# A fused attention and two-layer kernel: written order on all engines up to slot 20, weight tiles in two overlapped steps, constant products in the start

## The chip, the core and the metric

The kernel runs on one core of one Trainium2 chip. The metric is the device time of one launch in microseconds (us). The engines are TensorE (PE, matrix products; PEld is its loading of stationary operands), VectorE (DVE), ScalarE (ACT), GpSimd (POOL) and SyncE (SP), which here issues all transfers; SPq is SP's queue of transfers. Each engine works through its own list of instructions in order, and semaphores hold an instruction back until its inputs are written and its buffer is free.

## The reference

A linear attention is followed by a normalization and two layers. Token counts: 4 batches of 576 tokens, 8 heads of 64, so 2304 tokens of 512 numbers.

```python
kv  = np.einsum('bhsd,bhse->bhde', k, v)          # 64x64 per head, no softmax
out = np.einsum('bhsd,bhde->bhse', q, kv)
rms = np.sqrt(np.mean(out * out, axis=-1, keepdims=True) + 1e-06)
x   = (out / rms * g_norm)                        # to (2304, 512)

h = x @ w_in                                      # layer 1: 512 -> 2048
g = h * np.tanh(softplus(h))                      # mish
x = g @ w_out                                     # 2048 -> 512

h = x @ w_in2                                     # layer 2, same shapes
g = np.maximum(h, 0) + alpha * np.minimum(h, 0)   # a slope per hidden unit
return g @ w_out2
```

The weights of both layers come as 64-bit floats, everything else as 32-bit floats.

## The kernel before

**Blocks and slots.** The 2304 tokens are cut into blocks of 512, 256, 512, 512 and 512 (block 0 to block 4). Layer 1 takes the blocks in this order, layer 2 in the order 0, 2, 3, 4, 1. For each block the 2048 hidden units are done in 16 chunks of 128 (index j), so there are 2 x 5 x 16 = 160 steps, called slots: slots 0 to 15 are block 0 of layer 1, slots 16 to 31 block 1, and so on. In slot s, `slot` issues the first product of chunk s (`mm1`, 12 matmuls into the tile `h`), the activation of chunk s-1 (`mish` on ACT, or `prelu` on DVE in layer 2) and the second product of chunk s-4 (`mm2`, 12 matmuls added into the `acc` tiles; LAG = 4).

**Three matmuls for one.** Each product operand is split in a high part and a low rest. `three` (L121) multiplies high by high (L122), high by low (L123) and low by high (L124). So each operand is made in two operations: a copy to the high type on ACT (`xh` L306, `w` L381, `gh` L115) and a subtraction on DVE (`xl` L311, `w` L385, `gl` L118). In before the split of g (`g_split`) is issued directly behind the activation.

**Weight tiles.** A tile of 64-bit weights is loaded as pairs of 32-bit words into a staging buffer `ws` (`load_w`, L325 for `w_out`, L328 and L330 for `w_in`; three buffers). It is turned into a 32-bit tile `wf` by a scaling on ACT (`w_scale`, L336) and three operations on DVE, each reading the result of the one before (`w_bits`: L342, L343, L346); the text calls these three a bit build. Then come the high copy on ACT (`w_high`, L381) and the low subtraction on DVE (`w_low`, L385). `prep_w` issues the four steps of one tile. In slots 4 to 15 each slot prepares a tile of `w_in` (called w with its j) and one of `w_out` (u with its j), in the group `last`, at the end of the slot. The tiles c0 to c3 are the `w_in` tiles for j = 0 to 3, laid out as `w1first`.

**Attention.** The 512 columns of x are four pairs of heads. For block i and pair p: load of q (L175) and, for a new batch, of k and v (L153); `kv_pe` makes kv (L191), `kv_ev` copies its two 64x64 corners to SBUF (L199 on ACT, L200 on DVE); `t_pe` transposes q (L209, L211), `t_ev` copies it (L218, ACT); `o_pe` multiplies (L226). Block 0 then goes through a square (L240), a product with constants that gives the mean over each head (L244), a root on ACT (L249, L252) and three DVE operations. For blocks 1 to 4 the means of all four pairs are gathered, `rsqrt_ev` finds the reciprocal root by a bit trick and three Newton steps on DVE (twelve operations, L276 to L285, the last writes `yr`), and four broadcast products (`b_pe`, L290) and scalings (`b_ev`, L296) give x. The table `WHEN` puts these steps of block i+1 as `hook`s into half-slots of block i; the loads go to `pre`, two slots ahead of the transpose but not before slot 4.

**What sets the order.** Everything before slot 4 is under a manual schedule of all engines: the loads in the order of the string `FIRST` (p is k, v and q of a pair; c, w, u are weight tiles), then the steps of the string `START`, one letter for a step (k for kv, t for transpose, o for the output product, A, D, H, L for the four weight steps, P for `mm1`, x and y for the two halves of x, g for `mish`) and its indices. From slot 4 on only PE's order is the written one; on the other engines a scheduler with a model of times chooses, and it may place a later slot's instructions among those of the start.

## Time and profile before

| | us |
|---|---|
| median of 3 runs (912.61 to 913.68) | 912.66 |
| the profiled execution | 913.11 |
| its span, first to last instruction | 911.30 |
| PE busy in the span (95%) | 865.6 |
| DVE busy (48%) | 440.3 |
| ACT busy (31%) | 281.8 |
| POOL busy | 1.4 |
| read from and written to HBM | 52.44 and 9.44 MB |

The profile is of one execution. Its times count from the first instruction; the span leaves out 1.8 us that lie around it. Busy is the time in which an engine executes an instruction; waits are not in it. The profile page cuts the span into 40 slices of 22.8 us and gives the busy share of each in tenths: PE begins with 6, 4, 7, 8, 9, 7, 7 and stands at 9 from then on, so the time in which PE isn't busy lies in the first seven slices, some 160 us. The views by stretch, by wait and by instruction below go there.

### The profile page before, as it was taken

Reading aid. Unit: us, or ns where it says so; the run is one execution under the profiler, and the core shown is the slowest. Engines: PE = TensorE matmul, PEld = TensorE weight load, DVE = VectorE, ACT = ScalarE, POOL = GpSimd, SP = SyncE. Lnnn points to the kernel's source line nnn. Section 1 sums busy time; section 2 is a strip of 40 time slices with the busy share of each in tenths; the row PEclk is TensorE's granted clock in tenths of the full one; section 3 lists DMA queues with packets and bytes.
Section 4 is the critical chain, followed back from the end, with each engine's and each line's share of the span. In section 5 each row is a group of like instructions: output and inputs, shape, how many; then the busy total and the mean of one; then the engine's idle time right before and its main releaser. Section 6 shows DMA issues by size and latency. Waiting matters only on the chain.

```text
span 911.3 us, 10793 instructions
## 1 busy us (share of the span) xinstructions
PE 865.6 (95%) x4368; PEld 709.8 (78%) x4368; DVE 440.3 (48%) x760; ACT 281.8 (31%) x513; POOL 1.4 (0%) x11
## 2 busy tenths in 40 slices
PE   6478977999999999999999999999999999999998
PEld 3356766898887887788888888888888888888897
DVE  4277787125114413351677789544344433444444
ACT  2364654333322334232555344111112111111111
POOL 0000000000000000000000000000000000000000
PEclk9789998999999999999999999999999999999999
DMA  9604852340310003000454144011002000100010
GB/s 244 198 1 133 250 175 67 76 123 1 91 46 12 1 17 122 1 0 24 161 164 142 65 165 159 1 36 58 1 1 81 0 1 1 59 1 0 1 47 24
DMA packets 50753, 62.57 MB, mean 69 GB/s; under 512 B 19728, under 2 KB 41232, under 8 KB 50704
## 3 DMA queue, kind: packets, MB, share of 16 engines
q1 hardware_dynamic: 50704, 61.89, 22.5%
q8 instruction: 34, 0.56, 0.3%
q14 instruction: 15, 0.12, 0.0%
HBM read 52.44 MB, written 9.44 MB: 68 GB/s over the span
## 4 chain that ended last, share of the span: by engine, by line
PE 86%; DMA 6%; DVE 4%; SPq 2%; ACT 1%; issue 1%; DVEq 0%; ACTq 0%
PE acc L122 14%; PE h L122 14%; PE h L124 14%; PE acc L123 14%; PE h L123 14%; PE acc L124 14%; DMA ws<-in_moe_w_in_dram 2%; DMA ws<-in_moe_w_out_dram 2%; SPq L175 2%; PE ops L226 1%; PE kvps L191 1%; DMA v<-in_v_dram 1%; DMA q<-in_q_dram 1%; DVE wf L346 1%; DVE wf L343 1%
## 5 line engine op out<-in xcount | busy, mean ns | idle before, releaser
L118 DVE TENSOR_TENSOR gl<-n,gh 128x512 fp32r<-128x512 f32 (+1 forms) x160 | 102.0, 637 | 347.2 <-ACT gh L115 346.8
L115 ACT CAST gh<-n 128x512 fp32r<-128x512 f32 (+1 forms) x160 | 92.3, 577 | 384.8 <-PE acc L123 243.3
L122 PE MATMUL h<-xh,w 128*128 128x512 f32 (+1 forms) x480 | 180.9, 377 | 2.6 <-ACT w L381 2.6
L124 PE MATMUL h<-xh,w 128*128 128x512 f32 (+1 forms) x480 | 178.6, 372 | 0.6 <-DVE w L385 0.4
L123 PE MATMUL h<-xl,w 128*128 128x512 f32 (+1 forms) x480 | 178.2, 371 | 0.0
L122 PE MATMUL acc<-gh,w 128*128 128x512 f32 (+1 forms) x320 | 120.9, 378 | 0.4 <-ACT w L381 0.4
L124 PE MATMUL acc<-gh,w 128*128 128x512 f32 (+1 forms) x320 | 118.2, 369 | 0.0
L123 PE MATMUL acc<-gl,w 128*128 128x512 f32 (+1 forms) x320 | 118.1, 369 | 0.0
L122 PE MATMUL acc<-w,gh 128*128 128x512 f32 x288 | 112.2, 390 | 0.0
L123 PE MATMUL acc<-w,gh 128*128 128x512 f32 x288 | 112.2, 390 | 0.0
L124 PE MATMUL acc<-w,gl 128*128 128x512 f32 x288 | 112.0, 389 | 0.0
L122 PEld LDWEIGHTS h<-xh,w 128*128 128x128 f32 x480 | 91.4, 190 | 21.6 <-issue 3.4
L124 PEld LDWEIGHTS h<-xh,w 128*128 128x128 f32 x480 | 91.5, 191 | 17.5 <-DVE w L385 2.2
L123 PEld LDWEIGHTS h<-xl,w 128*128 128x128 f32 x480 | 91.6, 191 | 15.9 <-issue 0.5
L122 PEld LDWEIGHTS acc<-gh,w 128*128 128x128 f32 x320 | 60.6, 189 | 11.0 <-ACT w L381 0.7
L124 PEld LDWEIGHTS acc<-gh,w 128*128 128x128 f32 x320 | 60.5, 189 | 10.7 <-DVE w L385 0.4
L123 PEld LDWEIGHTS acc<-gl,w 128*128 128x128 f32 x320 | 60.6, 189 | 10.2 <-issue 0.5
L336 ACT ACTIVATE ws<-ws 128x512 f32<-128x512 f32 x64 | 43.3, 681 | 68.6 <-DMA ws<-in_moe_w_out_dram 37.2
L122 PE MATMUL h<-xh,w1first 128*128 128x512 f32 (+1 forms) x160 | 62.8, 392 | 1.3 <-ACT xh L306 1.3
L124 PEld LDWEIGHTS acc<-w,gl 128*128 128x128 f32 x288 | 54.1, 188 | 11.3
L122 PEld LDWEIGHTS acc<-w,gh 128*128 128x128 f32 x288 | 54.2, 188 | 10.9
L123 PE MATMUL h<-xl,w1first 128*128 128x512 f32 (+1 forms) x160 | 60.6, 379 | 2.2 <-DVE xl L311 2.2
(80 smaller groups left out, 845.8 us busy)
## 6 DMA issues: line engine op xcount, KB each, us to landing
ws<-in_moe_w_in_dram SPq DMA_DIRECT2D x32, 512.0 KB, 4.5
ws<-in_moe_w_out_dram SPq DMA_DIRECT2D x32, 512.0 KB, 3.5
k<-in_k_dram SPq DMA_DIRECT2D x16, 288.0 KB, 4.1
v<-in_v_dram SPq DMA_DIRECT2D x16, 288.0 KB, 4.3
out_dram<-osb SPq DMA_DIRECT2D x18, 256.0 KB, 2.4
x2d<-xs SPq DMA_DIRECT2D x8, 512.0 KB, 2.7
xs<-x2d SPq DMA_DIRECT2D x8, 512.0 KB, 4.2
q<-in_q_dram SPq DMA_DIRECT2D x16, 128.0 KB, 3.5
```

Of the source, the lines that this page charges most:

```text
L115: nc.scalar.copy(out=hi, in_=src)
L118: lo_eng.tensor_tensor(out=lo, in0=src, in1=f32(hi), op=ALU.subtract)
L122: nc.tensor.matmul(ps, lh, rh, start=start, stop=False)
L123: nc.tensor.matmul(ps, lh, rl, start=False, stop=False)
L124: nc.tensor.matmul(ps, ll, rh, start=False, stop=stop)
L175: nc.sync.dma_start(out=t[p0 : p0 + n, h, :, :], in_=q[b, 2 * p + h, s : s + C * n, :].rearrange("(p c) d -> p c d", c=C),)
L191: nc.tensor.matmul(ps[hs, hs], kt[:, h, j, :], vt[:, h, j, :], start=(j == 0), stop=(j == KVJ - 1))
L226: nc.tensor.matmul(cols(ps), kv_of(b, p), cols(qT), start=True, stop=True)
L336: nc.scalar.mul(high, high, 2.0**-112)
L343: nc.vector.scalar_tensor_tensor(out=si, in0=high, scalar=-0x80000000, in1=si, op0=ALU.bitwise_and, op1=ALU.bitwise_or)
L346: nc.vector.scalar_tensor_tensor(out=si, in0=high, scalar=3, in1=si, op0=ALU.logical_shift_left, op1=ALU.bitwise_or)
```

## The change

1. A constant `MANUAL` = 20: slots 4 to 19 are now issued inside the manual schedule of all engines; from slot 20 on, as before, only PE's order is written.
2. `prep_w` is cut in two: `w_begin` does scaling and bits of a tile and then ends the tile begun before it (`w_end`: high and low). In slots 4 to 15 the `w_in` tile is begun in a new group `mid` (after the activation, before `mm2`), the `w_out` tile in `last`; so the high and low of one tile stand behind the bits of the next.
3. `g_split` of a chunk is no longer issued behind its activation but one slot later, after `mm2`. `split` is gone (its two lines stand in `g_split`).
4. `START` and `FIRST` are written anew. In `START` PE steps and evacuations now have letters of their own (K and k, T and t, O, M, G), and W with a number issues so many matmuls of a constant 128x128 tile with itself (14 in all: W9, W2, W2 and one more); nothing reads their result. In `FIRST` pair 1 comes before tile c1 as before but pair 2 behind it; the load of `gcol` moves behind pair 1.
5. `kv_ev` copies both corners on DVE for block 0 and both on ACT for the others (before: one on each).
6. The loads of q, k and v of pairs 1 to 3 of a block are issued in the slot after the half-slot in which the previous pair's kv step stands, no longer two slots ahead of the transpose.

```diff
-FIRST = "p0 c0 p1 p2 c1 p3 c2 c3 w4 u0 w5 u1".split()
+MANUAL = 20
+FIRST = "p0 c0 p1 c1 p2 p3 c2 c3 w4 u0 w5 u1".split()
 START = """
-k0 t0 Ac0 o0 Dc0 s0 m0 Hc0 k1 l0 Lc0 n0 t1 f0 o1 k2 s1 x0 m1 Ac1 y0 l1 Dc1 P00 P01 P02 P03 n1 Hc1
...
+W9 K0 k0 W1 T0 t0 W2 Ac0 O0 Dc0 s0 W2 K1 M0 k1 Hc0 Lc0 T1 l0 t1 n0 O1 f0 K2 s1 x0 M1 k2 Ac1 y0 T2 l1
...
     def kv_ev(b, p):
         ps = at.pop(("kv", b, p))
-        nc.scalar.copy(out=kv_of(b, p)[:D, :D], in_=ps[:D, :D])
-        nc.vector.tensor_copy(out=kv_of(b, p)[D:, D:], in_=ps[D:, D:P])
+        for hs in (slice(0, D), slice(D, P)):
+            if b == 0:
+                nc.vector.tensor_copy(out=kv_of(b, p)[hs, hs], in_=ps[hs, hs])
+            else:
+                nc.scalar.copy(out=kv_of(b, p)[hs, hs], in_=ps[hs, hs])
...
+    begun = []
+    def w_end():
+        while begun:
+            w = begun.pop()
+            w_high(*w)
+            w_low(*w)
+    def w_begin(*w):
+        w_scale(*w)
+        w_bits(*w)
+        w_end()
+        begun.append(w)
...
-        g_split(kk, g)
+        gs[kk] = g
...
-            add(pre, max(h // 2 - 2, EARLY), load_q, i, p)
+            before = max((h - step + dk) // 2 + 1 if p else h // 2 - 2, EARLY)
+            add(pre, before, load_q, i, p)
...
-            add(last, j - 2, prep_w, 0, 1, j)
+            add(mid, j - 2, w_begin, 0, 1, j)
...
-            add(last, j + 2, prep_w, 0, 2, j)
+            add(last, j + 2, w_begin, 0, 2, j)
+            add(mid, j + 3, w_end)
...
             prelu(s - 1)
+        run(mid, s)
         run(fin, s)
         if s - LAG >= 0:
             mm2(s - LAG)
+        if s - 2 < K:
+            g_split(s - 2)
         run(hook, 2 * s + 1)
...
+    def warm(n):
+        ps = bank("acc3", "warm")
+        for _ in range(n):
+            nc.tensor.matmul(ps[:, :P], ones_bd, ones_bd, start=True, stop=True)
...
+        begun.append((0, 2, 1))
+        for s in range(EARLY, MANUAL):
+            slot(s)
     with tc.manual_schedule(engines={mybir.EngineType.PE}):
-        for s in range(EARLY, K + LAG):
+        for s in range(MANUAL, K + LAG):
             slot(s)
```

Three places show how instructions move. The first is ACT in the start, around the copy of the third transposed q (L218 before, L216 now), between the root of pair 1 and the high half of that pair's or the next pair's x. Before:

```order
L252 ACTIVATE u<-q 128x512
L381 CAST w1first<-wf 128x4x128
L336 ACTIVATE ws<-ws 128x512 x2
L218 COPY q<-tps 128x512
L336 ACTIVATE ws<-ws 128x512
L199 COPY kv_102<-kvps 64x64
L336 ACTIVATE ws<-ws 128x512
L306 CAST xh_346<-q 128x512
```

Now:

```order
L247 ACTIVATE q<-mps,epsb 128x512
L250 ACTIVATE u<-q 128x512
L216 COPY q<-tps 128x512
L238 ACTIVATE q<-ops 128x512
L379 CAST w1first<-wf 128x4x128
L304 CAST xh_349<-q 128x512
L334 ACTIVATE ws<-ws 128x512
```

Before, two scalings of staged weights stand ahead of the copy; now the copy stands right behind the root, and the scaling of the next tile comes after the high half of x.

The second place is SP, the transfers from slot 4 on: `w_out` and `w_in` tiles, and q (four pieces), k and v of block 1's pairs. Before:

```order
L325 DMA ws<-in_moe_w_out_dram 128x1024 x2
L328 DMA ws<-in_moe_w_in_dram 128x4x256
L175 DMA q<-in_q_dram 32x2x64 x2
L175 DMA q<-in_q_dram 96x2x64 x2
L153 DMA k<-in_k_dram 96x2x384
L153 DMA v<-in_v_dram 96x2x384
L328 DMA ws<-in_moe_w_in_dram 128x4x256
L325 DMA ws<-in_moe_w_out_dram 128x1024
```

Now:

```order
L323 DMA ws<-in_moe_w_out_dram 128x1024 x2
L326 DMA ws<-in_moe_w_in_dram 128x4x256 x2
L170 DMA q<-in_q_dram 32x2x64 x2
L170 DMA q<-in_q_dram 96x2x64 x2
L148 DMA k<-in_k_dram 96x2x384
L148 DMA v<-in_v_dram 96x2x384
L323 DMA ws<-in_moe_w_out_dram 128x1024
L326 DMA ws<-in_moe_w_in_dram 128x4x256
```

Before, a q stands between the first and the second `w_in` tile of this stretch (j = 6 and 7), and it was pair 2's, as the q of pairs 0 and 1 had been issued ahead of these rows; now both `w_in` tiles go first, and the q behind them is pair 1's.

The third place is DVE in block 0's last slots, around the reciprocal root of block 1 (L276 to L285 before, L274 to L283 now). Before:

```order
L276 TENSOR_SCALAR qT<-msps 128x256
L118 TENSOR_TENSOR gl<-n,gh 128x512
L342 TENSOR_SCALAR wf<-ws 128x512
L277 TENSOR_SCALAR qT<-qT 128x256
L385 TENSOR_TENSOR w_1063<-wf,w_1063 128x512
L343 SCALAR_TENSOR_TENSOR wf<-ws,wf 128x512
L281 TENSOR_TENSOR qT<-qT 128x256
L342 TENSOR_SCALAR wf<-ws 128x512
L346 SCALAR_TENSOR_TENSOR wf<-ws,wf 128x512
L282 SCALAR_TENSOR_TENSOR qT<-qT 128x256
```

Now:

```order
L447 TENSOR_TENSOR gl<-n,gh 128x512
L274 TENSOR_SCALAR qT<-msps 128x256
L275 TENSOR_SCALAR qT<-qT 128x256
L279 TENSOR_TENSOR qT<-qT 128x256
L280 SCALAR_TENSOR_TENSOR qT<-qT 128x256
L281 SCALAR_TENSOR_TENSOR qT<-qT 128x256
...
L283 SCALAR_TENSOR_TENSOR yr<-yr,neglo,qT 128x256
L340 TENSOR_SCALAR wf<-ws 128x512
L341 SCALAR_TENSOR_TENSOR wf<-ws,wf 128x512
L344 SCALAR_TENSOR_TENSOR wf<-ws,wf 128x512
L383 TENSOR_TENSOR w_1020<-wf,w_1020 128x512
```

Before, the steps of the root alternate with bit builds and low halves of weights; now its twelve steps stand in a row, and the three steps of a bit build too.

## Rows read from the trace of the kernel before

**Rows 1.** Windows: busy us (and instructions) per engine, granted clock, DMA share.

```profile
core 0: us, PE busy (x) PEld busy (x) DVE busy (x) ACT busy (x) POOL busy (x), PEclk, DMA share, GB/s
0.00:31.47 31.47, 21.91 (x140) 13.63 (x140) 14.74 (x51) 9.37 (x17) 1.43 (x11) 1.00 0.92 243
31.47:42.85 11.38, 0.00 (x1) 0.00 (x0) 0.00 (x0) 1.77 (x3) 0.00 (x0) 0.70 0.70 212
42.85:65.95 23.10, 18.50 (x84) 12.41 (x85) 15.15 (x25) 14.99 (x26) 0.00 (x0) 0.78 0.00 1
65.95:161.91 95.96, 81.41 (x449) 62.79 (x447) 74.69 (x144) 50.04 (x96) 0.00 (x0) 0.93 0.51 151
161.91:911.30 749.39, 743.78 (x3700) 620.93 (x3696) 335.75 (x542) 205.67 (x372) 0.00 (x0) 1.00 0.16 51
```

**Rows 2.** Waits of PE, whole span: total us, times, longest us.

```profile
PE kvps L191 <- ACT q L218: 11.4, 1, 11.4
PE bps L290 <- DVE yr L285: 11.1, 2, 9.2
PE kvps L191 <- DMA v<-in_v_dram: 5.2, 1, 5.2
```

**Rows 3.** Timeline, ACT around 41 us: start, length, instruction, [idle before it].

```profile
40.37 0.65 ACT L336 ACTIVATE ws<-ws 128x512 f32<-128x512 f32 x1 [12.21 <-DMA ws<-in_moe_w_out_dram]
...
42.23 0.57 ACT L218 COPY q<-tps 128x512 f32<-128x512 f32 x1
```

**Rows 4.** Chain that ended last, first 200 us: start, length, step.

```profile
12.59 8.19 DMA v<-in_v_dram
```

**Rows 5.** Waits of SP's queue, 0 to 160 us: total, times, longest.

```profile
SPq L175 <- PE tps L211: 48.3, 3, 31.7
```

**Rows 6.** Timeline of SP after that wait.

```profile
69.56 2.51 SPq L175 DMA_DIRECT2D q<-in_q_dram  x4
...
77.86 0.39 SPq L328 DMA_DIRECT2D ws<-in_moe_w_in_dram  x1
```

**Rows 7.** Timeline of PE, first matmul of slot 16.

```profile
161.91 0.39 PE L122 MATMUL h<-xh,w1first 128*128 128x256 f32 x1
```

**Rows 8.** Timeline of DVE, one bit build and the next one's start.

```profile
59.39 0.42 DVE L342 TENSOR_SCALAR wf<-ws 128x512 int32<-128x512 int32 x1
59.84 0.69 DVE L343 SCALAR_TENSOR_TENSOR wf<-ws,wf 128x512 int32<-128x512 int32 x1
60.57 0.69 DVE L346 SCALAR_TENSOR_TENSOR wf<-ws,wf 128x512 int32<-128x512 int32 x1
61.18 0.42 DVE L342 TENSOR_SCALAR wf<-ws 128x512 int32<-128x512 int32 x1
```

**Rows 9.** Timeline of PE, two products that give the means of a pair.

```profile
12.87 2.07 PE L244 MATMUL mps<-q,ones_bd 128*128 128x512 f32 x2 [0.69 <-ACT q L240]
...
48.61 1.13 PE L244 MATMUL mps<-q,ones_bd 128*128 128x512 f32 x2 [1.18 <-ACT q L240]
```

**Rows 10.** Timeline of PE after the wait for the root (`yr`).

```profile
142.09 0.63 PE L122 MATMUL h<-xh,w 128*128 128x512 f32 x1
142.52 0.63 PE L123 MATMUL h<-xl,w 128*128 128x512 f32 x1
...
145.64 0.40 PE L122 MATMUL h<-xh,w 128*128 128x512 f32 x1
145.88 0.39 PE L123 MATMUL h<-xl,w 128*128 128x512 f32 x1
```

**Rows 11.** Groups of DVE, 65.95 to 161.91: count | busy us, mean ns | idle before.

```profile
L281 DVE TENSOR_TENSOR qT<-qT 128x256 f32<-128x256 f32 x3 | 1.3, 418 | 0.0
...
L276 DVE TENSOR_SCALAR qT<-msps 128x256 f32<-128x256 f32 x1 | 0.4, 423 | 0.0
```

**Rows 12.** Transfers issued at 94.7 and at 106.8: count, size, us to landing.

```profile
ws<-in_moe_w_in_dram SPq DMA_DIRECT2D x1, 512.0 KB, 4.3
...
ws<-in_moe_w_in_dram SPq DMA_DIRECT2D x1, 512.0 KB, 5.5
```

More of the change, by code (lines that the diff above doesn't have):

```diff
@@ L111, in attn_moe_moe2 @@
     f32 = lambda t: t.bitcast(F32)
-    def split(hi_eng, lo_eng, hi, lo, src):
-        if hi_eng is nc.scalar:
-            nc.scalar.copy(out=hi, in_=src)
-        else:
-            hi_eng.tensor_copy(out=hi, in_=src)
-        lo_eng.tensor_tensor(out=lo, in0=src, in1=f32(hi), op=ALU.subtract)
     def three(ps, lhs, rhs, start, stop):
@@ L385, in w_low, with prep_w @@
         nc.vector.tensor_tensor(out=l, in0=s, in1=f32(h), op=ALU.subtract)
-    def prep_w(L, which, j):
-        for f in (w_scale, w_bits, w_high, w_low):
-            f(L, which, j)
-    hps, gt, acc = {}, {}, {}
+    begun = []
[9 more added lines that the diff above has]
+        begun.append(w)
+    def prep_w(*w):
+        w_begin(*w)
+        w_end()
+    hps, gs, gt, acc = {}, {}, {}, {}
     def at_slot(kk):
@@ L427, in m_tile, with g_split @@
         return mp.tile([P, T], dt, tag=nm, name=nm, bufs=bufs)
-    def g_split(kk, g):
+    def g_split(kk):
         T = at_slot(kk)[3]
+        g = gs.pop(kk)
         gh, gl = m_tile("gh", T, F32R), m_tile("gl", T, F32R)
-        split(nc.scalar, nc.vector, gh, gl, g)
+        nc.scalar.copy(out=gh, in_=g)
+        nc.vector.tensor_tensor(out=gl, in0=g, in1=f32(gh), op=ALU.subtract)
         gt[kk] = gh, gl
@@ L479, in load_x2 @@
         x2s[i, p], x2s[i, p + 1] = xs[:, :T], xs[:, T:]
-    pre, hook, fin, last = ({} for _ in range(4))
+    pre, hook, mid, fin, last = ({} for _ in range(5))
     def add(d, s, f, *a):
@@ L500, in attn_moe_moe2 @@
             if i in new_kv:
-                add(pre, max(h // 2 - 2, EARLY), load_kv, new_kv[i], p)
+                add(pre, before, load_kv, new_kv[i], p)
                 add(hook, h + dk, kv_pe, new_kv[i], p)
@@ L544, in slot @@
             mm2(s - LAG)
+        if s - 2 < K:
+            g_split(s - 2)
         run(hook, 2 * s + 1)
         run(last, s)
+    def warm(n):
+        ps = bank("acc3", "warm")
+        for _ in range(n):
+            nc.tensor.matmul(ps[:, :P], ones_bd, ones_bd, start=True, stop=True)
     code = {"c": 0, "w": 1, "u": 2}
     first = {
-        "k": lambda p: (kv_pe(0, p, "acc0"), kv_ev(0, p)),
-        "t": lambda p: (t_pe(0, p, "acc0"), t_ev(0, p)),
-        "o": lambda p: o_pe(0, p, f"acc{1 + p % 2}"),
+        "W": warm,
+        "K": lambda p: kv_pe(0, p, "acc0"),
+        "k": lambda p: kv_ev(0, p),
+        "T": lambda p: t_pe(0, p, "acc0"),
+        "t": lambda p: t_ev(0, p),
+        "O": lambda p: o_pe(0, p, f"acc{1 + p % 2}"),
         "s": s_ev,
-        "m": m_pe,
+        "M": m_pe,
         "l": m_ev,
@@ L566, in attn_moe_moe2 @@
         "g": mish,
+        "G": g_split,
     }
@@ L575, in attn_moe_moe2 @@
                 load_w(0, code[n[0]], int(n[1:]), True)
-            if n == FIRST[0]:
+            if n == "p1":
                 for h in range(2):
@@ L602, in attn_moe_moe2 @@
             if n[0] in "ADHL":
-                first[n[0]](0, code[n[1]], int(n[2:]))
+                w = (0, code[n[1]], int(n[2:]))
+                first[n[0]](*w)
             else:
                 first[n[0]](*(int(c) for c in n[1:]))
+        begun.append((0, 2, 1))
+        for s in range(EARLY, MANUAL):
+            slot(s)
     with tc.manual_schedule(engines={mybir.EngineType.PE}):
-        for s in range(EARLY, K + LAG):
+        for s in range(MANUAL, K + LAG):
             slot(s)
```

8 lines of the change are left out of this document (4 added, 4 removed).

## The prediction

> **What bounds the kernel now.** I began with the windows [rows 1]. From 161.91 us on TensorE (PE) is busy for 743.78 of 749.39 us: that stretch is matmul work and no order of other engines shortens it. The 161.91 us before it hold 121.8 us of PE work, and that is all a start-up change can reach. The waits of PE [rows 2] name three large items: one wait of 11.4 us for an ACT copy, one of 9.2 us (of 11.1) for the block-1 reciprocal root `yr`, 5.2 us for the first loads.
>
> The timeline around the first [rows 3] shows its real cause: PE waits for ACT's copy of the third transposed q, and that copy stands on ACT behind a weight scaling (L336) that waited 12.21 us for a `w_out` transfer. That tile belongs to a later slot; the order lists show that the scheduler set it into the hand-written start. Meanwhile the last q/k/v of block 0 were long there: the v of pair 3 was issued at 12.59 and landed 8.19 us later, at 20.8 [rows 4].
>
> The SP queue shows a third delay [rows 5]: a q load waited 31.7 us for a PE transpose, and the weight tile for j=7 was issued only at 77.86, behind it [rows 6]. So slots 4 to 15 began with weight tiles late, and VectorE (DVE), which needs about as long per slot as PE, ran 74.69 of 95.96 us there [rows 1].
>
> **The change, part by part.** Marks are slot 4's first matmul (65.95, the edge of a window in rows 1) and slot 16's, 161.91 [rows 7].
>
> *Start, up to slot 4.* With ACT in written order no scaling of a later slot stands ahead of a copy, so the 11.38 us stretch with an idle PE goes. What is late next? Data first: pair 3 is complete at about 21. Then DVE: from about 19 us its list, in written order, holds for pairs 1 to 3 and the tiles c1 to c3: three bit builds, three lows, three normalizations, three x lows and two kv copies. By the distances of the starts in [rows 8] a build is 0.45+0.73+0.61 = 1.79. What else has 512 columns I price by these steps: a low (of a weight, of x or of g) 0.61 to 0.7, a normalization, three dependent operations, 3 x 0.73 = 2.2, a pair of kv copies one short step, 0.5. The sum is 5.4+2.0+6.6+2.0+1.0 = 17 us, to 36 or 37. The low half of x3 is the last of it and releases the last twelve first-layer matmuls, 12 x 0.24 = 2.9 us [rows 10]: slot 4 starts at about 41 instead of 65.95, **25 us less**. Bounds: 26 (no wait left in that list) and 20 (PE's in-order chain of kv, transpose, o and mean products at the lower clock for all four pairs).
>
> *Warm-up products.* 14 products of 128x128 on PE. Before, none exists; by the mean product of 512 columns, 2.07 us at 12.87 and 1.13 at 48.61 [rows 9], a quarter of that is 0.5 or 0.28 us. Nine of them, 2.5 to 4.5 us, stand where PE waits 5.2 us for the first v [rows 2]; they may overrun that by some 0.5 us, on a path that then waits for transfers, so nothing. Five more stand in waits like the 0.69 us at 12.87. What they may give: the two mean products tell that PE ran its first 30 us at the lower of its two levels (1.2 GHz), though the profile writes a granted 1.00 there [rows 1]. At the higher one each pair's PE steps take about half. It is a gain only where PE, not DVE, is last, which after the step above it mostly isn't: 0, bounds -3 and +1, already in the ends of the first term.
>
> *kv copies.* Block 0's go to DVE, the others' to ACT: eight small copies less on DVE (at most a short step each, 3.6 us), beside other work: 0.
>
> *Load order (q and k/v of block 1).* In the written order q of pair 1 stands behind the j=7 tile, q of pair 2 behind j=9, and q of pair 2 finds the buffer that pair 0's transpose frees in slot 4, so the 31.7 us wait goes. But in the built program each `w_in` tile waits for the build of the `w_in` tile before it (the buffer freed first is handed out first), so SP holds the q of pair 2 until tile 8 is built, in the middle of slot 6, and its transpose comes right after the matmuls of slot 7. I walk it below.
>
> *Slots 4 to 15.* Before they take 95.96 us: 14.55 idle, some 14 matmuls at the lower level (0.43 instead of 0.24, 2.7 us in all [rows 10]), 78.6 us of work. After, DVE from its first build of slot 4's tile has 24 tiles (w4 to w15, u0 to u11) of 1.79+0.6 = 57.4 us, twelve `gl` of 0.61 (7.3), the block-1 root with twelve operations (the kinds from L276 to L285, 1.3 busy for each of three of them, 0.4 for a small one [rows 11]; 5.1 in all, 5.6 with gaps) and block 1's four x (3.5): 74 us, from 37 to 111. PE from 41 to 120. Both are nearly full, so each wait of one for the other is lost. Walking the two lists by these pitches: (a) `gh` waits for the second product of its slot, since its buffer is read there, then come `gl`, build u, low w, low u, build w: 5.4 us, within a slot of 5.45 to 6.9; (b) a `w_in` tile lands 4.3 us after its issue [rows 12], then scaling (0.65 [rows 3]) and two bit steps (1.2): 6.2 us from build to build, within a slot while attention steps lengthen it (slots 4 to 9), 0.7 us over it in slots 10 to 13, which the waits of (d) and (e) cover; (c) q of pair 2 issues at about 64, lands at 69, PE is ready at 65.3: 3.7 idle and 1.8 at the lower level after it; (d) in slot 10 the root stands in a row on DVE, between `gl` and the build of u8, so low w12 comes at 105 where PE wants it at 100: 4.5, and 1.5 at the lower level; (e) block 1's four broadcast products and slot 15's weights wait 3 us behind DVE. With 0.5 of small waits that is 78.6+15 = 93.6, less about 2 since the last x tiles overlap slot 15: 91.5, **4.5 us less**. Bounds: 78.6 (PE never waits, -17) and 104 ((b) paces every slot at 8 us, +8).
>
> A rule weighed against this: of the two long bit operations the one whose result the next operation reads takes 0.73 us, the one with another tile's work behind it 0.61 [rows 8]; the written order gives up that mixing, 0.12 us per tile, 3 us over 24 tiles. The Trainium skill (VectorE: DVE Perf Modes, "The DRAIN you can't avoid") says that a semaphore between chained operations costs nothing extra, as the pipeline drains anyway. The rows speak against that by 0.12 us; by the page the DVE sum would be 71 instead of 74.
>
> *From slot 16 on.* The order on PE is the same, and DVE (336 us busy of 749) has room: 0. Bounds: -3.6 (the 1.9 us of the second root's wait and the low level after it gone) and +3 (another such wait, since the split of g now stands after the second product).
>
> Sum: -25 - 4.5 + 0 = -29.5. The profiled execution took 913.11 us (span 911.30), 0.45 above the median of the runs: 913.1 - 29.5 = 883.6, or **883** on the median's footing.
>
> **Rivals.**
> 1. *The two queues mesh.* Items (c) to (e) vanish in the slack: slot 16 at 120, saving 25 + 17 = 42, 871. For: the sums of PE and DVE (79 and 74) allow it. Against: one root on DVE already cost 9.2 us before.
> 2. *The weight path paces slots 4 to 15.* One buffer for all `w_in` tiles, the transfer shared with q and k/v (5.5 instead of 4.3 in one case [rows 12]), scaling behind `gh` on ACT: 8 us per slot, 41 + 104 = 145, saving 17: 896.
> 3. *Slower: TensorE stays at the lower level through slots 4 to 15.* Before, the waits of 11.4 and 9.2 us were each followed by work at the lower level [rows 1, 10]. If every slot has such a wait, the 78.6 us of work take 157: slot 16 at 41 + 157 + 14 = 212, and 50 us are lost: 963. It decides from 30 us of work run at half rate, between four and five of the twelve slots. Against: after such a wait about seven matmuls ran slow, 1.4 us in all. The Trainium skill (TensorE: Matmul & The Clock Gate, "HAM oscillation") describes such a kernel, which falls back at every tile's load wait; the trace shows the fall after single waits, none of a repeated kind.
> 4. *The change doesn't do what it says:* the scheduler puts tiles of slots from 20 on ahead of the written ones, as it did with L336. The order lists of the built program show none; then 900 at best. Too small to count apart from 2.
>
> **Chances and range.** Forecast 0.70 (873 to 892), rival 1 0.13, rival 2 (with 4) 0.13, rival 3 0.04. To hold 8 in 10 the range reaches to the points of both neighbours, 870 to 897, and leaves out their far halves and rival 3, 0.17 in all. Faster 0.95, within 0.2% (1.8 us, about what a measurement here can tell) 0.01, slower 0.04.
>
> **What would show it.** ACT: the copy of the third q right after its transpose, before 30 us. PE: slot 4's first matmul near 41, slot 16's near 132. SP: no wait over 10 us before slot 8, but the q of pair 2 issued after tile 9, and a PE wait at its transpose. DVE: the root's operations in a row, and PE waiting in slot 12. Granted clock: a dip after each of these two waits. Wrong if PE is idle for over 5 us between 6 and 40 other than for transfers, if slot 4 starts after 46, or if new waits stand after slot 16.

## The result, and the profile after

| | before | after |
|---|---|---|
| median of the runs | 912.63 us | 887.15 us |
| lowest and highest | 912.54 to 913.68 | 885.32 to 889.0 |
| the profiled execution, its span | 913.11, 911.30 | 887.53, 885.7 |

The ratio is 0.9718, with a 95% interval of 0.9697 to 0.974: the change saves 25.5 us. The forecast was 883, with a range of 870 to 897. The span lost 25.6 us, and the windows tell where. They answer to [rows 1], now cut at PE's first transpose, at slot 4's first matmul and at slot 16's. The columns are the same: busy us and instructions of PE, PEld, DVE, ACT and POOL, the granted clock, the DMA share and GB/s.

```profile
0.00:12.97 12.97, 5.02 (x44) 4.63 (x45) 4.83 (x36) 1.28 (x1) 1.43 (x11) 0.93 0.89 234
12.97:45.04 32.07, 29.41 (x209) 19.92 (x209) 24.13 (x42) 20.78 (x35) 0.00 (x0) 0.92 0.76 216
45.04:137.86 92.82, 82.38 (x450) 63.85 (x449) 73.45 (x131) 49.92 (x100) 0.00 (x0) 0.94 0.51 149
137.86:885.70 747.84, 742.27 (x3700) 619.36 (x3696) 340.72 (x546) 210.97 (x386) 0.00 (x0) 1.00 0.17 52
```

Up to slot 4 the time fell from 65.95 to 45.04 (20.9 us), slots 4 to 15 from 95.96 to 92.82 (3.1 us), everything from slot 16 on from 749.39 to 747.84 (1.55 us). The prediction had 25, 4.5 and 0.

The 11.4 us wait of [rows 2] for ACT's copy of the third q is gone. That copy stands right behind the root, with no idle time ahead of it (timeline of ACT, answering to [rows 3]):

```profile
26.11 0.63 ACT L250 ACTIVATE u<-q 128x512 f32<-128x512 f32 x1
26.64 0.57 ACT L216 COPY q<-tps 128x512 f32<-128x512 f32 x1
```

What PE waits for now, over the whole span (total us, times, longest us; answers to [rows 2]):

```profile
PE tps L207 <- issue: 6.3, 1, 6.3
PE tps L209 <- DMA q<-in_q_dram: 3.1, 1, 3.1
PE h L117 <- ACT w L379: 2.1, 1, 2.1
...
PE bps L288 <- DVE qT L294: 1.9, 1, 1.9
PE bps L288 <- DVE yr L283: 1.9, 1, 1.9
PE warm L572 <- DVE ones_bd L615: 1.4, 1, 1.4
PE acc L117 <- ACT n L453: 1.4, 1, 1.4
PE h L119 <- DVE w L383: 1.2, 1, 1.2
```

All but the first are short. But for the wait for the second root (`yr`, block 2's, behind slot 16) and the one at the constant products, those shown lie in slots 4 to 15; the rows left out are two of 1.0 us and smaller ones. The first is new and the longest, and its row names no engine that it waits for, only "issue". It stands in PE's timeline at 12.97, ahead of the very first transpose:

```profile
5.32 0.92 PE L186 MATMUL kvps<-v,k 96*64 96x64 f32 x24 [0.21 <-DMA v<-in_v_dram]
6.17 0.49 PE L572 MATMUL warm<-ones_bd 128*128 128x128 f32 x2
12.97 1.97 PE L207 MATMUL tps<-ident,q 128*64 128x128 f32 x16 [6.32 <-issue]
```

DVE's timeline at the same time gives the reason:

```profile
5.29 0.15 DVE L629 TENSOR_TENSOR neglo<-neglo,ident 128x1 f32<-128x1 f32 x1
12.31 0.15 DVE L630 TENSOR_SCALAR gneg<-gcol 128x1 f32<-128x1 f32 x1 [6.88 <-DMA gcol<-in_g_norm_dram]
12.42 0.46 DVE L196 COPY kv<-kvps 64x64 f32<-64x64 f32 x2
```

The product kv was done at 6.2. Its two copies to SBUF are now both on DVE, and they stand there behind `gneg`, a constant made from `gcol`. Point 4 of the change moved the two tiny `gcol` transfers behind pair 1's loads; they were issued at 5.2 and landed at 12.3, in the queue of the large ones. The transpose uses the bank that kv occupies until the copies are done, so DVE, ACT and PE all stood still for 6 us. PE paid for it twice: the kv product ahead of the wait took 0.92 us, the higher of TensorE's two levels, and the transposes behind it 1.97, the lower one (1.09 in the next pair).

### The profile page after: what moved, and what is told of

Same layout as the page of the kernel before. It is cut to its first block, busy times and chain, and to the rows that moved or that the text cites. A ratio compares the mean times of both kernels' runs of the same rounds, so it can differ in the third digit from the quotient of the medians.

```text
span 885.7 us, 10841 instructions
## 1 busy us (share of the span) xinstructions
PE 859.1 (97%) x4396; PEld 707.8 (80%) x4396; DVE 443.1 (50%) x752; ACT 283.0 (32%) x521; POOL 1.4 (0%) x11
## 4 chain that ended last, share of the span: by engine, by line
PE 92%; DVE 3%; ACT 2%; DMA 2%; issue 1%; SPq 0%; DVEq 0%
PE acc L117 15%; PE acc L118 14%; PE acc L119 14%; PE h L117 14%; PE h L119 14%; PE h L118 14%; PE ops L224 2%; PE kvps L186 2%; DMA ws<-in_moe_w_in_dram 1%; PE tps L209 1%; DVE wf L341 1%; DVE wf L344 1%; PE mps L242 0%; DMA v<-in_v_dram 0%; PE bps L288 0%
## 5 line engine op out<-in xcount | busy, mean ns | idle before, releaser
L117 PEld LDWEIGHTS acc<-gh,w 128*128 128x128 f32 x320 | 60.9, 190 | 12.3 <-ACT n L453 1.8
L119 PEld LDWEIGHTS acc<-gh,w 128*128 128x128 f32 x320 | 60.8, 190 | 10.9 <-DVE w L383 0.4
L118 PEld LDWEIGHTS acc<-gl,w 128*128 128x128 f32 x320 | 61.0, 191 | 10.3 <-issue 0.5
L117 PEld LDWEIGHTS acc<-w,gh 128*128 128x128 f32 x288 | 54.1, 188 | 10.7
L118 PEld LDWEIGHTS acc<-w,gh 128*128 128x128 f32 x288 | 54.1, 188 | 10.7
L117 PE MATMUL h<-xh,w1first 128*128 128x512 f32 (+1 forms) x160 | 59.9, 375 | 0.0
```

Source lines behind the costliest of these rows:

```text
L117: nc.tensor.matmul(ps, lh, rh, start=start, stop=False)
L118: nc.tensor.matmul(ps, lh, rl, start=False, stop=False)
L119: nc.tensor.matmul(ps, ll, rh, start=False, stop=stop)
```

## The experiments

All are edits of the kernel after, and each was timed against the kernel before. The "stretch" is the time from slot 4's to slot 16's first matmul in the profiled execution. "PE idle" is the stretch less PE's busy time in it, that is, what PE waited. "Slow" counts the matmuls of 512 columns in the stretch that took over 0.55 us, where the others took some 0.4. The two columns tell a wait that an edit removed from a lower clock that an execution happened to miss.

| run | edit, in words | median us | ratio, 95% interval | slot 4 | stretch | PE idle | slow |
|---|---|---|---|---|---|---|---|
| after | | 887.15 | 0.9718, 0.9697 to 0.974 | 45.04 | 92.82 | 10.4 | 21 |
| e1_gcol_early | `gcol` loaded behind pair 0 | 882.71 | 0.9661, 0.9641 to 0.9681 | 37.65 | 94.42 | 10.3 | 28 |
| e2_manual_to_4 | written order up to slot 4 only | 900.72 | 0.9867, 0.9844 to 0.9891 | 55.46 | 94.60 | 14.6 | 10 |
| e3_no_warm | no constant products | 889.07 | 0.9735, 0.9715 to 0.9754 | 44.52 | 93.73 | 9.9 | 27 |
| e4_one_step | weight tiles in one step | 905.08 | 0.9908, 0.9891 to 0.9926 | 44.02 | 109.95 | 24.0 | 28 |
| e5_gcol_no_warm | e1 without constant products | 883.31 | 0.9684, 0.9668 to 0.9699 | 40.70 | 92.38 | 10.9 | 15 |
| e6_gcol_q_early | e1, q of pair 2 earlier | 880.4 | 0.9653, 0.9634 to 0.9671 | 38.31 | 92.19 | 10.7 | 15 |
| e7_gcol_root_split | e1, root in three parts | 882.57 | 0.9672, 0.9658 to 0.9685 | 37.65 | 93.39 | 11.8 | 12 |
| e8_all_three | e6, e7 and earlier broadcasts | 883.01 | 0.9675, 0.9656 to 0.9694 | 37.98 | 94.48 | 11.2 | 21 |
| e9_two_more_stages | e1, two staging buffers for w_in | 876.25 | 0.9585, 0.9563 to 0.9607 | 37.68 | 87.57 | 7.9 | 8 |
| e10_two_bit_steps | e1, a bit operation left out | 873.22 | 0.9559, 0.9537 to 0.9582 | 38.08 | 85.69 | 5.0 | 14 |
| e11_stages_and_three | e8 and e9 | 876.25 | 0.959, 0.9568 to 0.9611 | 37.55 | 87.75 | 7.5 | 12 |
| e12_waits_one_by_one | e9, three local edits | 874.43 | 0.9579, 0.9564 to 0.9594 | 37.95 | 85.64 | 7.4 | 0 |

### The load that moved with the rest: e1

```diff
-            if n == "p1":
+            if n == "p0":
                 for h in range(2):
                     nc.sync.dma_start(out=gcol[...], in_=g_norm...)
```

> The kernel after, with one edit: the two small gcol transfers stand behind pair 0's loads again (as before the change), not behind pair 1's. Theory A: in the kernel after, DVE's list is held at gneg until gcol lands (12.31 us), the first kv copies stand behind it, and PE has 6.3 us without work; with gcol early gneg comes at 6 to 7 us, everything up to slot 4 moves by 5 to 6 us (slot 4's first matmul at 39 to 40 instead of 45.0), and the time is 881 to 882.5. Theory B: transfers or DVE's sum of work bound the start anyway; slot 4 moves by under 2 us and the time stays at 885 to 888.

Measured: 882.71 us, and slot 4's first matmul at 37.65, 7.4 us earlier. DVE's rows at the place of the 6.88 us wait:

```profile
6.26 0.15 DVE L630 TENSOR_SCALAR gneg<-gcol 128x1 f32<-128x1 f32 x1 [0.81 <-DMA gcol<-in_g_norm_dram]
6.60 0.46 DVE L196 COPY kv<-kvps 64x64 f32<-64x64 f32 x2 [0.18 <-PE kvps L186]
```

Theory A holds for the start, which gained more than its 5 to 6 us. Of the 7.4 us, 4.3 reach the profiled time (883.27 against 887.53): slots 4 to 15 took 1.6 us more and the rest 1.6 us more. Neither is a wait that the edit made: PE waits as long in the stretch as in after (10.3 against 10.4) and has 28 slow matmuls against 21; for the rest see the last section.

### What the written order of the later slots gave the start: e2

```diff
-MANUAL = 20
+MANUAL = 4
```

> The kernel after with MANUAL = 4: START, FIRST, the two-step preparation and the later split of g stay, only the written order of ACT, DVE and SP from slot 4 on is undone. In its order list five scalings of later weight tiles stand again among ACT's steps of the start; DVE's list of the start is unchanged. Theory A: the 11.4 us wait of before was such a misplaced scaling, so one or more waits of ACT of 5 to 15 us come back, PE waits for an ACT copy, slot 4 starts at 55 to 66, the time is 897 to 908. Theory B: the new START list is what gained, and the written order of the later slots little; slot 4 at 45 to 48, the time 886 to 890.

Measured: 900.72 us, slot 4 at 55.46. ACT's timeline has the old picture again, now a pair later: one scaling stands ahead of the fourth copy.

```profile
30.30 0.69 ACT L247 ACTIVATE q<-mps,epsb 128x512 f32<-128x512 f32 x1
38.25 0.66 ACT L334 ACTIVATE ws<-ws 128x512 f32<-128x512 f32 x1 [7.27 <-DMA ws<-in_moe_w_out_dram]
38.81 0.61 ACT L250 ACTIVATE u<-q 128x512 f32<-128x512 f32 x1
39.33 0.57 ACT L216 COPY q<-tps 128x512 f32<-128x512 f32 x1
```

PE's product with that copy waited 6.9 us. DVE's written start is the same as in after, so theory A holds for the 10.4 us by which slot 4 is later: they are this wait and 4.5 us more of PE busy time up to slot 4, at a granted clock of 0.78 from 13 us on where after has 0.92, less 0.9 us by which the wait for `gneg` is shorter. In the stretch the wait for the block-1 root is there again with 10.3 us, and PE waits 14.6 us in all against 10.4; that the stretch is only 1.8 us longer is in part due to fewer slow matmuls (10 against 21). So more than half of what the written order of slots 4 to 19 brings lies in the start, by keeping later work out of it. The other half of the start's 20.9 us comes from the rest of the change: with `MANUAL` = 4 slot 4 is still 10.5 us earlier than in before. Which of its parts gave that (the new `START`, the load order, the copies of kv on one engine) no run separates.

### The constant products: e3 and e5

```diff
-W9 K0 k0 W1 T0 t0 W2 Ac0 O0 Dc0 s0 W2 K1 M0 k1 ...
+K0 k0 T0 t0 Ac0 O0 Dc0 s0 K1 M0 k1 ...
```

> The kernel after without its 14 constant products. Theory A (the prediction's): they are worth nothing, since DVE's list paces the start; slot 4 at 44.5 to 46, the time 886.5 to 888.5. Theory B: PE's chain of transposes and products paces the start (from 13 to 31 us PE has gaps of 1 us only), and without the constant products it runs at the lower level up to about 29 us, as before; each of four pairs takes 2 to 3 us longer, slot 4 at 51 to 55, the time 893 to 897.

Measured: 889.07 us, slot 4 at 44.52 (45.04 with them): theory A for the start. The time lies 0.6 us above its range, with 27 slow matmuls in the stretch against 21, and 1.6 us more from slot 16 on, of which the last section tells. But the reason is not the one given there. In both kernels PE is at the lower level after the wait of some 6 us for `gneg` (the first transposes take 1.97 us in both), so that wait undoes what the products ahead of it had given. e5 takes the wait away.

> gcol early (as in e1_gcol_early) and without the 14 constant products. Theory A: the constant products were worth nothing in the kernel after because the 6 us wait for gneg gave the time back anyway; with that cover gone PE runs the pairs at the lower level (kv step 1.55 instead of 0.92, transposes 1.97 instead of 1.09, o 2.05 instead of 1.10, means 2.07 instead of 1.13), 3.4 us per pair for two or three pairs, until it has worked long enough: slot 4 at 42 to 47 instead of 37.65, the time 887 to 892. Theory B: DVE's list paces the start at either level; slot 4 at 37.5 to 39, the time 882 to 884.

Measured: 883.31 us, slot 4 at 40.70 against 37.65 with the products: 3.05 us, the price of the first pairs at half rate (kv step 1.55 instead of 0.92, transposes 1.98 instead of 1.09), until the rate doubles at about 17 us. Neither theory's number: A expected 4 to 9 us, B under 1.5. In the whole time it doesn't show, 883.31 against 882.71 with overlapping intervals, since the stretch of e5 happened to be 2.0 us shorter, with fewer slow matmuls in it (15 against 28) and no less waiting. So the products give 3 us in the start where no wait follows them, and nothing in the kernel after.

### Two steps for a weight tile: e4

```diff
-            add(mid, j - 2, w_begin, 0, 1, j)
+            add(last, j - 2, prep_w, 0, 1, j)
...
-            add(last, j + 2, w_begin, 0, 2, j)
-            add(mid, j + 3, w_end)
+            add(last, j + 2, prep_w, 0, 2, j)
```

> The kernel after with each weight tile prepared in one go again (scaling, bits, high, low, at the end of the slot), all else as after. Theory A: DVE then waits some 0.6 us at each low for ACT's copy of the same tile, 24 tiles, 14 us on an engine that is nearly full in slots 4 to 15; half of it or more shows, the stretch of slots 4 to 15 takes 100 to 107 us instead of 92.8, the time 894 to 901. Theory B: DVE has that slack, other waits (q of pair 2, the root) set the pace; 92 to 95 us, the time 886 to 890.

Measured: 905.08 us, a stretch of 109.95, more than theory A's upper end. The waits of DVE in the stretch:

```profile
DVE gl L447 <- ACT gh L446: 15.0, 13, 6.2
DVE w L383 <- ACT w L379: 13.7, 20, 0.7
```

The second row is theory A's term, twenty waits of at most 0.7 us. But the edit also moved the `w_in` tile from the middle of its slot to the end: its load is then issued 7.5 to 8.8 us after the one before (13 in two places), where after has 6.1 to 7.5 (9.5 and 11.5 in two places). PE waits 13.5 us more than in after (24.0 against 10.4) and is busy for 3.6 us more (86.00 against 82.38), at a granted clock of 0.91 against 0.94. How much of the 17 us is the overlap, how much the place, and what causes the first row was not taken apart; so the run shows what preparing a tile in one go at the end of a slot costs, and not what the two steps alone are worth.

### Taking waits away one at a time: e6, e7 and e8

The prediction had priced the stretch as five separate waits, (a) to (e). These runs remove them, each on top of e1.

e6 issues the q of pair 2 a slot earlier:

```diff
-            add(pre, before, load_q, i, p)
+            add(pre, max(before - 1, EARLY) if i == 1 and p == 2 else before, load_q, i, p)
```

> gcol early, and the q of block 1's pair 2 issued one slot earlier, ahead of the tiles u5 and w8 instead of behind them. Theory A: the 3.0 us wait of PE at the transpose in slot 7 is that load, held behind tile w8 on SP; the wait goes, with the lower level behind it (1 to 2 us): slots 4 to 15 take 90 to 91.5 instead of 94.4, the time 878 to 880. Theory B: the tile w8 that now comes later pays it back (its build, and so slot 8, is late by 2 to 4 us); the time stays at 881.5 to 883.5.

e7 cuts `rsqrt_ev` for block 1 in three functions; `rsqrt_0` has the setup and the first Newton step, `rsqrt_1` the third step, ACT's copy and `yr`:

```diff
-        add(hook, h, rsqrt_ev, i)
+        add(hook, h, rsqrt_0, i)
+        add(hook, h + 1, newton, i)
+        add(hook, h + 2, rsqrt_1, i)
```

> gcol early, and block 1's reciprocal root cut in three: two setup operations and the first Newton step where the whole root stood, the second step a half-slot later, the third with ACT's copy and yr another half-slot later. Theory A: the waits of PE in slot 12 (2.1 for the high half of w12, 1.2 for its low half) come from the root's twelve operations in a row on DVE and from ACT's copy of yr that waits for them in front of the high half of w12; they go, yr comes 3 to 5 us later where 10 us are free; slots 4 to 15 take 89.5 to 92 instead of 94.4, the time 878 to 880.5. Theory B: the work of DVE is the same and the wait only moves to the next tile or to the b products; the time stays at 881.5 to 883.5.

e8 has both edits and the broadcast products a half-slot earlier:

```diff
-WHEN = {1: (8, 3, 1, 2, 4, 4), 2: (-2, 5, 1, 2, 4, 6), 3: (0, 5, 1, 2, 4, 4), 4: (0, 5, 1, 2, 4, 4)}
+WHEN = {1: (8, 3, 1, 2, 4, 3), 2: (-2, 5, 1, 2, 4, 6), 3: (0, 5, 1, 2, 4, 4), 4: (0, 5, 1, 2, 4, 4)}
```

> gcol early, q of pair 2 early, the root in three parts, and the four broadcast products of block 1 one half-slot earlier. Theory A: the waits of slots 7, 12 and 14 (3.0, 3.3, 1.9 us) are separate and their savings add, with the lower level behind them: slots 4 to 15 take 83 to 87 us, the time 871 to 876. Theory B: DVE and the weight path are so full that a wait removed shows up at the next tile; the stretch stays above 90 us, the time above 878.

Measured: 880.4, 882.57 and 883.01 us, stretches of 92.19, 93.39 and 94.48 against 94.42. Every edit did away with its wait or most of it, and each time another came. The longest wait of PE in e1 is the one for the q of pair 2:

```profile
PE tps L209 <- DMA q<-in_q_dram: 3.0, 1, 3.0
```

In e6 it is gone, and the next step of the same pair waits as long for its v:

```profile
PE kvps L186 <- DMA v<-in_v_dram: 3.0, 1, 3.0
```

In e8 that has shrunk to 1.7, but the first broadcast product waits for `yr`, which before it did not:

```profile
PE bps L296 <- DVE yr L291: 4.1, 1, 4.1
```

In e7 the wait of 2.1 for w12 is gone, and 1.3 for `yr` and 1.1 more at another broadcast product came in its place. The table has it in one column: PE waits 10.7, 11.8 and 11.2 us in the stretch, against 10.3 in e1. Where a stretch is shorter, it has fewer slow matmuls (15 and 12 against 28 in e6 and e7). In this sense theory B holds in all three, though e6's time lies between the two ranges; it is 2 us below e1's with overlapping intervals. So the waits could not be taken away one at a time. e8 is the weakest of the three tests, since its own edits move the broadcast products earlier and `yr` later, which lengthens that wait by design.

### What sets the pace: e9, e10 and e11

SP's timeline of the kernel after shows the candidate, the loads of `w_in` tiles in slots 8 to 12:

```profile
86.42 0.38 SPq L326 DMA_DIRECT2D ws<-in_moe_w_in_dram  x1
...
92.86 0.37 SPq L326 DMA_DIRECT2D ws<-in_moe_w_in_dram  x1
...
98.98 0.37 SPq L326 DMA_DIRECT2D ws<-in_moe_w_in_dram  x1
...
110.44 0.37 SPq L326 DMA_DIRECT2D ws<-in_moe_w_in_dram  x1
...
116.60 0.37 SPq L326 DMA_DIRECT2D ws<-in_moe_w_in_dram  x1
```

They follow each other at 6.1 to 6.4 us, the 6.2 us of item (b), and at 11.5 where the root stands on DVE. (Those before them, at 55.34, 61.99, 69.38, 78.90 and 86.42, follow at 6.7 to 9.5.) A load that waits on SP also holds the q, k and v behind it. e9 gives these tiles buffers of their own; no memory is added, as the places are those where u14 and u15 will be kept. The three old buffers are then left to the `w_out` tiles.

```diff
-        s = room("ws", I32, 2 * DM) if early else stage("ws", I32, 2 * DM)
+        if L == 0 and which == 1 and j >= 6:
+            s = wp.tile([P, 2 * DM], I32, tag=f"w2{14 + j % 2}", name="ws")
+        else:
+            s = room("ws", I32, 2 * DM) if early else stage("ws", I32, 2 * DM)
```

> gcol early, and the w_in tiles w6 to w15 of layer 1 staged in two buffers of their own (the places where u14 and u15 will be kept, free until slot 16), not in the three buffers shared with the w_out tiles. Nothing else is changed. After e6 to e8, in which a wait taken away came back at another place, two theories of what holds slots 4 to 15 at 92 to 94 us. Theory W (the weight path): each w_in tile is loaded only when the one before has been built, 6.1 us from load to load at best and longer when SP is held; with two buffers the loads run ahead, the q and v loads behind them on SP too, and the stretch falls to 82 to 87 us, the time 870 to 876. Theory D (DVE): DVE's list of some 74 us of work with its waits for ACT in it sets the pace; loads that come earlier change little, 91 to 94 us, the time 881 to 884.

e10 instead shortens DVE's work, by leaving out the third bit operation (L344) of the layer-1 tiles from w4 and u0 on:

> gcol early, and the third bit operation of each layer-1 tile from w4 and u0 on left out (28 to 32 operations of 0.7 us; the weights are then wrong by their low bits, the order and the waits stay). DVE has 17 us less to do in slots 4 to 15; the load-to-load time of the w_in tiles falls by 0.7 us a slot at most. Theory D: the stretch falls from 94.4 to 80 to 84 us, the time 869 to 873. Theory W: it falls by under 6 us, to 88 to 92, the time 876 to 881.

e11 has the edits of e8 on top of e9:

> The two more staging buffers of e9 together with the edits of e8 (q of pair 2 early, root in three parts, broadcast products a half-slot earlier). Theory W: with the loads ahead the waits are separate items, their savings add now; the stretch takes 80 to 84 us, the time 867 to 873, below e9 by 2 to 5 us. Theory D: no better than e8 by over 2 us, 880 to 884.

Measured: e9 876.25 us with a stretch of 87.57, e10 873.22 with 85.69, e11 876.25 with 87.75. The window of the stretch in e1:

```profile
37.65:132.07 94.42, 84.12 (x450) 65.13 (x449) 73.62 (x131) 49.99 (x100) 0.00 (x0) 0.93 0.51 153
```

In e9:

```profile
37.68:125.25 87.57, 79.70 (x449) 61.85 (x448) 73.22 (x131) 49.48 (x100) 0.00 (x0) 0.98 0.54 166
```

In e10:

```profile
38.08:123.77 85.69, 80.69 (x450) 63.30 (x449) 57.23 (x107) 49.31 (x100) 0.00 (x0) 0.96 0.58 168
```

By its numbers theory W is nearly met in e9 (87.57 against its 82 to 87, 876.25 against 870 to 876), and theory D is out. But the columns divide the 6.9 us: PE's waits fall by 2.4 us (10.3 to 7.9), since those for q and v are gone altogether, and its busy time by 4.4 (84.12 to 79.70), since 20 of 28 slow matmuls are. The buffers thus remove the transfers from what PE waits for, and the larger part of the gain is the clock. It isn't the chance of one execution, as all five runs of e9 take 874.64 to 876.44 us and all of e1 880.31 to 883.27; why the slow matmuls went, the runs don't show.

In e10 DVE has 16 us less to do, and the stretch falls by 8.7: nearer to theory D's numbers than to W's (85.69 and 873.22, where D had 80 to 84 and 869 to 873). PE's waits fall by 5.3 us, more than twice as much as in e9, though the loads are held as in e1; the wait for q is still 2.4 us, while those for slot 12's tile and at the broadcast products shrink. So a large part of PE's waits hangs on DVE's list. The run doesn't tell its length from its place in the loop from load to load, as the shortened builds are part of both.

e11 meets neither theory: theory W wanted 2 to 5 us less than e9, theory D 880 to 884. With loads ahead, the three edits bring nothing (87.75 against 87.57), but the broadcast product waits 4.1 us for `yr` in e11 as in e8, a wait which e9 doesn't have and the edits brought. What e9 leaves is a list on DVE that is 84% busy (73.22 of 87.57) and whose order decides which tile comes late.

### The waits that are left: e12

On top of e9, the activation of chunk 3 (g3) moves ahead of the high half of w5, the halves of w12 are issued ahead of the root, and `b_two` makes two broadcast products in one bank:

```diff
-... g2 Dw5 Au1 Hw5 Du1 Lw5
+... g2 Dw5 Au1 g3 Hw5 Du1 Lw5
...
+        if i == 1:
+            add(hook, h, lambda: w_end())
         add(hook, h, rsqrt_ev, i)
...
+            if i > 1:
+                add(hook, h + db + p, b_pe, i, p)
+            elif p % 2 == 0:
+                add(hook, h + db + p, b_two, i, p)
```

> e9_two_more_stages and three local edits, each for one wait that e9 still shows: the high and low half of w12 are issued ahead of the root instead of behind it (waits of 1.65 and 1.17 us in slot 12); the broadcast products of block 1 are made two at a time, in the two halves of one bank (1.06, 0.60 and 1.91 us); the activation of chunk 3 stands ahead of the high half of w5 on ACT (1.39 us). In e11 the root in parts made yr late and nothing was won; here no step of the root is later by more than the low half in front of it. Theory A: with loads ahead of need the waits left are separate, local orders on DVE and ACT: 5 to 7 us of these 7.8 go, the stretch of slots 4 to 15 falls from 87.6 to 80.5 to 83, the time to 869 to 872. Theory B: DVE's list as a whole is what is late, and what is taken from one place shows at the next: 86 to 88 us, the time 874 to 877.

Measured: 874.43 us, a stretch of 85.64. Its waits of PE in the stretch:

```profile
PE h L119 <- DVE w L394: 2.8, 2, 1.7
PE bps L296 <- DVE qT L302: 2.1, 1, 2.1
PE acc L117 <- ACT w L390: 1.7, 1, 1.7
PE h L117 <- ACT w L390: 0.6, 1, 0.6
PE kvps L186 <- ACT qT L216: 0.2, 1, 0.2
```

The window of the stretch:

```profile
37.95:123.59 85.64, 78.23 (x449) 60.67 (x448) 73.30 (x131) 49.74 (x100) 0.00 (x0) 1.00 0.56 169
```

The waits sum to 7.4 us, those of e9 to 7.9. The wait of 1.4 at the start and the waits for w12 are gone, and u8, w13 and w15 are late instead. Of the 1.9 us that the stretch gained, 1.5 are slow matmuls that didn't occur (none against 8), and 0.5 are waits, where theory A wanted 5 to 7. So theory B holds, with a stretch 0.4 us below its range: what is taken from one place shows at the next. That it is DVE's list as a whole which is late fits this and e10; no run that changes only the list's length shows it alone. e9 and e12 can't be told apart by their times (0.9585 and 0.9579, intervals overlapping). Both beat the kernel after: e9 by 1.4% (0.9585 to 0.9718).

## Why the prediction was right, and where it wasn't

**The start, -25 forecast, -20.9 measured.** The cause was right: e2 shows that a later scaling on ACT holds a copy, and in after, without it, the 11.4 us are gone. The size of DVE's list was right too. From the build of c1 to the low half of x3 it takes 25.51 to 42.24 in after and 18.14 to 34.89 in e1, without idle time, 16.7 us, where the sum was 17; the first-layer matmuls behind it take 2.8 (2.9 forecast). The step that failed is the list's beginning, "from about 19 us". It began at 25.5, since `gneg` waited for a load that the change had moved. The prediction named the load order of pairs and weight tiles, and left out the one load in that list which is 0.2 KB small. Without this, as e1 shows, slot 4 would have started at 37.65, earlier than the 41 on record (whose own sum, 19 + 17 + 2.9, is 39). So the record's 41 stands between two errors of opposite sign. That PE idled for 6.3 us here is near to the prediction's own sign of being wrong: a wait of over 5 us, which a transfer ended, but by way of DVE.

The prediction has DVE last and PE waiting for it. The traces show both lists ending together. DVE's list in after, its first row and the low half of x3:

```profile
25.51 0.42 DVE L340 TENSOR_SCALAR wf<-ws 128x512 int32<-128x512 int32 x1
...
41.55 0.69 DVE L309 TENSOR_TENSOR xl<-q,xh 128x512 fp32r<-128x512 f32 x1
```

PE at the same time, the last matmul before the twelve that read x3 and the first of them:

```profile
42.09 0.39 PE L119 MATMUL h<-xh,w1first 128*128 128x512 f32 x1
42.32 0.39 PE L117 MATMUL h<-xh,w1first 128*128 128x512 f32 x1
```

PE has no idle time from 35.75 to slot 4, so a shorter list on DVE alone would not have brought slot 4 forward from there.

**Warm-up products, 0 with -3 at best.** Right in after, by 0.5 us (e3), but by the cover of the wait for `gneg` and not for the reason given, that DVE is last. Where that wait doesn't undo them (e5), they bring the 3 us of the bound.

**Slots 4 to 15, -4.5 forecast, -3.1 measured.** 91.5 us against 92.82. The items: (b) 6.2 us from load to load, 6.1 to 6.4 in the trace where nothing else holds it; (c) q of pair 2 issued behind the load of tile 9, which waits for the build of tile 8, PE waiting 3.06 (3.7 forecast) at the place named, in slot 7; (d) in slot 12 PE waits 2.1 and 1.2 for w12 (4.5 forecast); (e) 1.9 for a broadcast product (3 forecast). All waits of PE sum to 10.4 us, where the items and small waits summed to 11.7. The 21 slow matmuls cost some 4.1 us by PE's busy time (82.38, against 78.23 in e12, which has none; 3.3 forecast), but none of them follows the wait of (c), where 1.8 us were forecast. In (d) the trace has a detail that the walk missed: ACT's copy for `yr`, which waits for DVE's last Newton step, stands ahead of the high half of w12, so the high half is late too:

```profile
97.60 0.62 ACT L446 CAST gh<-n 128x512 fp32r<-128x512 f32 x1 [0.15 <-PE acc L119]
104.35 0.40 ACT L282 CAST yr<-qT 128x256 fp32r<-128x256 f32 x1 [6.12 <-DVE qT L281]
104.66 0.66 ACT L334 ACTIVATE ws<-ws 128x512 f32<-128x512 f32 x1
105.22 0.61 ACT L379 CAST w<-wf 128x512 fp32r<-128x512 f32 x1
```

The sizes and places were right, but adding them up as separate costs was not right as a cause. e6 to e8 remove (c), (d) and part of (e), and PE waits as long as before. The prediction set (b) aside as covered by (d) and (e). e9, which takes (b) away, does away with (c) and leaves (d) about as long (2.8 us) and (e) longer (3.6), so (b) stands behind (c); what stands behind (d) and (e) is by e10 and e12 DVE's list, as far as they show it.

**From slot 16 on, 0 forecast, -1.55 measured.** This part takes 749.2 to 749.5 us in before, e1, e2, e3, e7 and e9 and 747.8 to 748.1 in after and the other runs, whatever the edit: it is the clock after the wait for the second root, below. Here the forecast gained 1.55 us by luck.

**The sum.** Against the forecast the start took 4.0 us more, slots 4 to 15 took 1.3 more and the rest 1.55 less. So the number came out by a mechanism that was right in its first part, and in its second by sizes that fit while their cause was another.

**The rivals.** Rival 1 (the queues mesh, 871) is not what the kernel after does; e9 and e12 come near it with other buffers. Rival 2 (the weight path paces) has an error in its sum: twelve slots at 8 us are 96 and not 104, so that slot 16 would start at 137 and the time be 888. That is nearer to what was measured (137.86 and 887.15) than the forecast's 883, and the time can't tell the two apart. Nor can the pitch: from 55.34 to 116.60 the `w_in` loads follow each other at 7.7 us on average, and the slots take 7.7 each. What tells is e9, where the loads run ahead and 2.4 of PE's 10.3 us of waits go: the weight path is a part of the pace, and not the whole. Rival 3 (the lower level throughout) did not occur: 0.94 granted in the stretch, as 0.93 before. Nothing of rival 4 shows in ACT's rows: the copy stands right behind the root. One sign failed without harm: SP waited 13.1 us for a build before it issued the load of tile 7 at 55.34, where no wait over 10 us was expected before slot 8.

**The rule weighed against the change.** In after a bit operation followed by its reader starts 0.73 us ahead of it, and one followed by an operation on another tile 0.61:

```profile
46.15 0.69 DVE L341 SCALAR_TENSOR_TENSOR wf<-ws,wf 128x512 int32<-128x512 int32 x1
46.88 0.69 DVE L344 SCALAR_TENSOR_TENSOR wf<-ws,wf 128x512 int32<-128x512 int32 x1
47.49 0.69 DVE L447 TENSOR_TENSOR gl<-n,gh 128x512 fp32r<-128x512 f32 x1
```

Two rows of the start take 0.72 though the next operation reads another tile (26.76 to 27.48, 32.58 to 33.30). The Trainium skill (VectorE: DVE Perf Modes, "The DRAIN you can't avoid") says that a semaphore between chained operations costs nothing extra; by these rows a dependent neighbour comes 0.12 us later. What giving up the mixing cost in time, no run shows: the busy time of DVE in the stretch (74.69 before, 73.45 after) counts the operations and not the distances between them.

## What to carry to other kernels

An engine in written order waits at the first instruction whose data are late, however small; so when loads are reordered, ask of each load, the tiny constants too, what stands in line behind its first reader. When several short waits add up to a stretch, remove one: if another comes in its place, look for what paces them, here one staging buffer's way from load to build to next load and, as far as the runs show, DVE's whole list. Before crediting an edit with a shorter stretch, split the difference into waits and busy time: of the 6.9 us that the buffers of e9 gave, 2.4 were waits and 4.4 the clock. And a written order pays first by what it keeps out: half of this start's gain was later work that no longer stood ahead of a copy.

## What the runs showed of the hardware

The same wait is followed by slow matmuls in one run and not in another. The wait for the second root is 1.9 us long in all profiles, and slow matmuls follow it in before, e1, e2, e3, e7 and e9 and not in the others. The 10 us in which it ends were granted 0.83 in e1 (window of PE's and the other engines' busy time, columns as above):

```profile
182.07:192.07 10.00, 9.05 (x57) 8.70 (x58) 6.35 (x10) 3.91 (x9) 0.00 (x0) 0.83 0.01 2
```

The same 10 us in the kernel after were granted 1.00:

```profile
187.86:197.86 10.00, 9.05 (x70) 8.80 (x71) 6.90 (x11) 4.32 (x10) 0.00 (x0) 1.00 0.01 2
```

The difference is the 1.6 us by which their last parts differ. In slots 4 to 15 the wait for q was followed by 7 slow matmuls in e1 and by none in after, and in e12 four waits of 1.1 to 2.1 us were followed by none at all (0 slow matmuls, clock 1.00), while in after one of 1.9 us was followed by 8. What decides this the runs don't show. Groups of 5 to 14 slow matmuls at some 0.2 us each are worth 1 to 3 us each time, and the four runs of after go with it: the slowest (889.0) has the lowest mean granted clock, 0.987, the fastest (885.32) the highest, 0.991. So edits of 2 us are told apart by the waits in the traces here, and hardly by the times.

In the start the granted clock was written as 1.00 in e5, while kv steps of 1.55 and transposes of 1.98 us show the lower rate: there the durations tell the level, not the column.
